# Linear attention and two dense stages on one core: queries of two halves through ScalarE and GpSimd, low part of y through TensorE in four halves

## The chip, the cores and the metric

The kernel runs on one core of a Trainium2 chip. The metric is the device time of one execution in microseconds (us). The kernel before took 769.47 us, the median of three runs (768.39, 769.47 and 771.44 us). A profiled execution of its own took 767.55 us.

## The reference

Three stages follow each other. The first is a gated linear attention, a recurrence over 768 steps for 4 batches and 8 heads of 48 dimensions:

```python
for t in range(S):
    state = alpha[:, :, t, :, None] * state + np.einsum('bhd,bhe->bhde', k[:, :, t], v[:, :, t])
    y[:, :, t] = np.einsum('bhd,bhde->bhe', q[:, :, t], state)
```

Its output, as 3072 tokens of 384 values, goes through a dense stage of 2048 hidden units with a rational function (`h = x @ w_in`, `g = P(h) / Q(h)`, `g @ w_out`), and then through one of 1024 hidden units with `h * softmax(h)`, a layer norm and `@ w_out`. Everything is float32.

## The kernel before, in words

**Numbers as two parts.** TensorE takes most operands as a pair: a rounded high part (`fp32r`) and the rest, the low part. A product of two such pairs takes three matmuls. So weights, activations and the attention's output y are all split: ScalarE copies the value to the high part, and another engine subtracts that from the value.

**The recurrence in chunks.** The 768 steps are cut into 6 chunks of 128. A *half* i is two of the four batches in one chunk, so there are 12 halves; chunk c has halves 2c and 2c+1. In a half, P is the running product of alpha from the chunk's start, and R is a scaled running product back from its end. The keys are multiplied by R and the queries by P. Then scores (line 421, tile `sc`), a causal mask (line 429 on GpSimd), and y as scores times v plus queries times the state (line 445, tile `y` in PSUM) follow, and last the state's update (tile `u`, line 486, and `Sbd`, lines 490 to 501).

**The first two halves** (`NPE = 2`) are prepared by `a_turn` (line 354): TensorE turns alpha, keys and queries by matmuls with the identity into PSUM (line 364). VectorE makes the scans for P (line 375) and R (line 379, with `zero` as its addend), and multiplies keys by R (line 383) and queries by P (line 384), each as one 128x512 instruction that reads PSUM. It does this for two groups p, so there are two of each per half. Later halves are prepared by `a_dve` (line 301), by VectorE's transposes (lines 291, 296), two scans (lines 309, 318) and products; there the queries are multiplied on GpSimd (line 336).

**y to the dense stage.** At the end of `a_pe` (lines 468 to 472) y lies in two PSUM tiles, of 512 and of 256 columns. For each, ScalarE copies the high part (line 471) and VectorE subtracts it from y, which gives the low part (line 472). All 12 halves do this, so there are 24 such subtractions. The PSUM tiles of the attention share two slots (tag `at`), and so the next tile that needs a slot waits until the last reader of an older one is done. Before halves 0 and 1 can update the state, `a_back` (line 393, tile `kp`) takes such a slot.

**The weights** of the first dense stage come in as pairs of 32-bit words (they are 64-bit in memory) and VectorE makes float32 of them in three instructions (lines 540, 543, 544), into a PSUM or SBUF buffer and then `ft`. ScalarE copies the high part (line 550) and GpSimd subtracts (line 551). This work, for four groups of hidden units, runs from the start of the kernel until about 139 us.

**The first dense stage** takes 16 units of hidden columns per chunk, 96 units in all. A unit u is `m_up` (9 matmuls, line 595; its function on ScalarE, VectorE and GpSimd, lines 600 to 629) and, four units later, `m_down` (9 matmuls, line 641). The PSUM tile `hp` of a unit has three slots. In the same loop, in pieces, run the halves from 2 on: the later halves are prepared and calculated while TensorE works on the units. The second dense stage (lines 709 to 799) comes behind this.

**What sets the order.** The program is written as one stream; a scheduler places it on the engines' queues by dependencies and a model of durations. Each engine then runs its queue strictly in order. `issue_after` adds, for instructions of the block on the same engine as the one named, an edge behind that one. At line 836 the preparation of half 2 is traced behind `marks[0, 1]`, which is the second subtraction of half 0 (line 472), a VectorE instruction:

```python
            with tc.issue_after(marks[0, 1].ins):
                _run(a_prep(2))
```

Other users of `issue_after` (lines 854 and 859 to 861) name instructions of the units. Before the loop the program is written in this order: loads of halves 0 and 1 with two pieces of the first weight group, `a_turn(0)`, `a_pe(0)`, `a_turn(1)`, `a_pe(1)`, the rest of that group, `clear()`, the second weight group, the preparation of half 2. All transfers are issued on SyncE's queue.

Of the kernel before, what the change touches and what calls it, by code (L numbers as in the profile page):

```python
# [7 lines left out]
F32 = mybir.dt.float32  # L8
F32R = mybir.dt.float32r
I32 = mybir.dt.int32  # L10
I64 = mybir.dt.int64
BF16 = mybir.dt.bfloat16
AF = mybir.ActivationFunctionType
ALU = mybir.AluOpType
# [5 lines left out]
def _view(ap, off, dims):  # L20
    return bass.AP(ap.tensor, ap.offset + off, [list(ap.ap[0])] + [list(d) for d in dims])
# [9 lines left out]
def kernel(  # L31
# [15 lines left out]
    nc = tc.nc  # L47
# [5 lines left out]
    CH = 128  # L53
# [9 lines left out]
    NPE = 2  # L63
# [90 lines left out]
    def network(fast):  # L154
# [7 lines left out]
        if fast:  # L162
            att = tc.tile_pool(name="att", bufs=1, side="right")
            ap_ = att.__enter__()
            ps_a = tc.tile_pool(name="ps_a", bufs=2, space=PSUM, side="right")
            ps_ap = ps_a.__enter__()
            ident = ap_.tile([128, 128], F32, name="ident")
            nc.gpsimd.memset(ident, 0.0)
            nc.gpsimd.affine_select(
                out=ident, in_=ident, pattern=[[-1, 128]], compare_op=ALU.not_equal, fill=1.0, base=0, channel_multiplier=1  # L170
            )
            zero = ap_.tile([128, CH], BF16, name="zero")
            nc.vector.memset(zero, 0.0)
            NB6 = 6
            PER = CH + 1
            QW = 4 * CH + 2
            d1 = ap_.tile([128, NB6 * PER + 1], BF16, name="d1")
            d2 = ap_.tile([128, NB6 * PER], F32, name="d2")
            alT = ap_.tile([128, NB6 * PER + 2], F32, name="alT")
            qks = ap_.tile([128, B, QW], F32, name="qks")  # L180
            kns = ap_.tile([128, B * 192 + 16], F32, name="kns")
            Sbd = ap_.tile([128, 2, B * 2, 2 * D], F32, name="Sbd")
            vns = ap_.tile([128, B * 256], F32, name="vns")

        def clear():
            nc.gpsimd.memset(d1, 0.0)
            nc.gpsimd.memset(_view(d1[:], 0, [[PER, NB6 + 1]]), 1.0)
            nc.gpsimd.memset(d2, 0.0)
            nc.vector.memset(alT[:, 0:1], 0.0)

# [35 lines left out]
        def half(i):  # L226
            if i not in halves:
                halves[i] = Half(i)
            return halves[i]

        marks = {}
# [3 lines left out]
        def watch(i, ra):  # L235
            jk = ap_.tile([128, 16 * D], BF16, name="jk", tag="qk")
            nc.scalar.activation(
                jk, ra[:, :16 * D], AF.Relu, bias=lim[:, 0:1], scale=-1.0, accum_out=bad[:, 2 * i:2 * i + 1]
            )

        def watch_end(i, end):
            jk = ap_.tile([128, 16], F32, name="jk2", tag="jk2")
            nc.scalar.activation(
                _view(jk[:], 0, [[end.shape[2], end.shape[1]], [1, end.shape[2]]]), end, AF.Relu, bias=lim[:, 1:2],
                accum_out=bad[:, 2 * i + 1:2 * i + 2],
            )
# [107 lines left out]
        def a_turn(i):  # L354
            hf = half(i)
            ra, rk, rq = raws.pop((i, "ra")), raws.pop((i, "rk")), raws.pop((i, "rq"))
            watch(i, ra)

            def turn(raw, p):
                t = (ps_hp if i < 2 else ps_ap).tile([128, B, CH], F32, name="tp", tag="h" if i < 2 else "at")  # L360
                for r in range(4):
                    for j in range(2):
                        o = (2 * p + j) * 192 + 48 * r
                        nc.tensor.matmul(
                            _view(t[64 * j:64 * j + 64], r, [[CH, B], [4, 32]]), lhsT=raw[:, o:o + 64], rhs=ident,
                            start=True, stop=True, skip_group_check=True,
                        )
                return t

            for p in range(2):  # L370
                al = turn(ra, p)
                P = ap_.tile([128, B, CH], F32, name="Pp", tag="P")
                R = ap_.tile([128, B, CH], F32, name="Rp", tag="qk")
                for b in range(B):
                    nc.vector.tensor_tensor_scan(P[:, b, :], al[:, b, :], zero, 1.0, ALU.mult, ALU.add)
                nc.vector.tensor_scalar(hf.end[p], P[:, :, CH - 1], P_MIN, None, ALU.max)
                nc.vector.reciprocal(R[:, :, CH - 1], hf.end[p])
                for b in range(B):
                    nc.vector.tensor_tensor_scan(
                        R[:, b, :CH - 1][:, ::-1], al[:, b, 1:][:, ::-1], zero[:, :CH - 1], R[:, b, CH - 1:],  # L380
                        ALU.mult, ALU.add,
                    )
                nc.vector.tensor_tensor(hf.k[p], turn(rk, p), R, ALU.mult)
                marks[i, p, 0] = nc.vector.tensor_tensor(hf.q[p], turn(rq, p), P, ALU.mult)
                yield
            watch_end(i, hf.ends[:, :, :, 0])

# [17 lines left out]
        def a_enter(i):  # L405
            if i < NPE:
                v_load(i)
                yield from a_turn(i)
            else:
                yield from a_move(i)  # L410

        def a_pe(i):
            c, bp = divmod(i, 2)
            vt = vts.pop(i)
            hf = half(i)
            A = {}
            for p in range(2):
                sc = [ps_ap.tile([128, B, CH], F32, name="sc", tag="at") for j in range(2)]
                for x in range(B):
                    for j in range(2):  # L420
                        nc.tensor.matmul(  # L421
                            sc[j][:, x, :],
                            lhsT=hf.k[p][64 * j:64 * j + D, x, :], rhs=hf.q[p][64 * j:64 * j + D, x, :],
                            start=True, stop=True,
# [13 lines left out]
            y2 = [ps_ap.tile([128, n, 2 * CH], F32, name="y", tag="at") for n in (2, 1)]  # L438
# [12 lines left out]
            for x in range(2):  # L451
                if c:
                    for hp in pairs:
                        g, p = divmod(hp, 2)
# [5 lines left out]
                for part in ((0, 1, 3), (2,)):  # L460
                    for hp in pairs:
                        g, p = divmod(hp, 2)
# [6 lines left out]
            for z, n in enumerate((2, 1)):  # L469
                hi, lo = (xt[:, 2 * z:2 * z + n, w, 256 * bp:256 * bp + 256] for w in range(2))  # L470
                nc.scalar.activation(hi, y2[z], AF.Copy)
                marks[i, z] = nc.vector.tensor_tensor(lo, y2[z], hi.bitcast(F32), ALU.subtract)
            yield
            if i >= NPE:
                yield
# [5 lines left out]
            for x in range(B):  # L481
                for p in range(2):
                    for j in range(2):
                        o = 192 * x + 96 * p + 48 * j
                        n = 256 * x + 128 * p + 64 * j
                        nc.tensor.matmul(
                            u[64 * j:64 * j + 64, 2 * x + p, :], lhsT=hf.kn[:, o:o + 64], rhs=vt[:, n:n + D],
                            start=True, stop=True, skip_group_check=True,
# [328 lines left out]
        if fast:  # L817
# [11 lines left out]
            take(pre, PRE[3])  # L829
            nc.gpsimd.memset(Sbd, 0.0)  # L830
            _run(a_turn(0), a_pe(0), a_turn(1), a_pe(1), pre)
            clear()
            pre = w1_group(1)
            take(pre, NA)
# [29 lines left out]
        def half_steps(i):  # L864
            gp = a_pe(i)
            gd = chain(a_prep(i + 1), a_move_qk(i + 1) if i + 1 >= NPE else iter(()), a_load(i + 2, ("ra", "rk")) if i + 2 < NH and i + 1 >= NPE else iter(())) if i + 1 < NH else iter(())
            while True:
                with pin(GP):
                    a = next(gp, "end")
                with pin(GS):  # L870
                    b = next(gd, "end")
                    if b != "end":
                        b = next(gd, "end")
                if a == "end" and b == "end":
                    if i + 1 < NH:
                        _run(a_enter(i + 1))
                        if i + 2 < NH and i + 1 < NPE:
                            _run(a_load(i + 2))
                    return
                yield  # L880
# [6 lines left out]
        for u in range(NU + LAG):  # L887
            c, f = divmod(u, NF1)
            now[0] = u
            if f % (NF1 // 2) == LATE and u < NU:  # L890
                _run(side)
                i = 2 * c + 2 + f // (NF1 // 2)
# [75 lines left out]
    def recurrence():  # L968
# [70 lines left out]
        sb.__exit__(None, None, None)  # L1039

    network(True)
    wide = nc.values_load(flag, min_val=0, max_val=1)
    with tc.If(wide > 0):
        recurrence()
        network(False)
# [30 lines left out]
```

## Time and profile before

| what | us |
|---|---|
| median of three runs | 769.47 |
| the profiled execution, its own time | 767.55 |
| its span, from the first to the last instruction | 765.8 |
| TensorE busy in the span | 726.4 |
| VectorE busy | 624.1 |
| ScalarE busy | 535.9 |
| GpSimd busy | 360.5 |

The profiled execution lies around its span by 1.75 us. In the rows, PE is TensorE's matmuls, PEld its loading of weights, DVE is VectorE, ACT is ScalarE, POOL is GpSimd, SP or SPq is SyncE's queue; L472 is line 472. A duration in the timeline runs until an instruction has fully ended, and the next one on the same engine may begin a little before that; so the step from one start to the next is the better price of an instruction in a queue that never waits.

### The profile page before, as it was taken

What the parts mean: (1) busy time and instruction counts of PE and PEld (TensorE: products, weight loads), DVE (VectorE), ACT (ScalarE), POOL (GpSimd) and SP (SyncE); (2) the same over time, 40 slices, a digit from 0 to 9 for tenths busy, and PEclk for the clock granted to TensorE, in tenths of its full rate; (3) what the DMA queues carried; (4) which work ended last, traced back from release to release, by engine and by line L of the source; (5) the groups of instructions that cost most, each with busy time, mean ns of one, the idle gap of its engine ahead of it and who ended that gap; (6) DMA issues with size and microseconds to landing.
All of it is one profiled execution on the core that took longest, in us unless ns stands there. A gap on an engine that the chain in (4) does not pass through costs nothing.

```text
span 765.8 us, 13905 instructions
## 1 busy us (share of the span) xinstructions
PE 726.4 (95%) x4976; PEld 606.0 (79%) x4976; DVE 624.1 (81%) x1111; ACT 535.9 (70%) x984; POOL 360.5 (47%) x306
## 2 busy tenths in 40 slices
PE   4775999999999999999999999999999999999996
PEld 4664777788888888877787878888888989988996
DVE  5999999879899999898989976568877787777730
ACT  2245877788888887897879798888875564645631
POOL 3256887766555455354444434422253334442422
PEclk9857899999999999999999999999999999999998
DMA  7995356357746584738462460910026264351552
GB/s 174 272 277 167 88 174 151 104 83 210 168 159 142 152 180 136 161 104 193 126 157 70 161 124 1 342 71 1 0 84 149 74 146 108 105 126 47 128 136 62
DMA packets 87278, 101.74 MB, mean 133 GB/s; under 512 B 34464, under 2 KB 63136, under 8 KB 87200
## 3 DMA queue, kind: packets, MB, share of 16 engines
q1 hardware_dynamic: 87008, 100.41, 49.9%
q8 instruction: 41, 0.67, 0.4%
q10 hardware_dynamic: 192, 0.36, 0.2%
q14 instruction: 37, 0.30, 0.1%
HBM read 60.59 MB, written 27.56 MB: 115 GB/s over the span
## 4 chain that ended last, share of the span: by engine, by line
PE 65%; DVE 20%; issue 5%; DMA 4%; ACT 3%; SPq 2%; POOL 0%; DVEq 0%; POOLq 0%; ACTq 0%
PE x2p L641 17%; PE hp L595 17%; PE op L787 13%; PE h L716 13%; PE y L445 2%; DMA lent<-in_moe_w_in_dram 2%; DVE w L624 2%; PE sc L421 2%; DVE hp L625 2%; SPq L267 2%; DVE p L626 1%; DVE ft L544 1%; DVE p L621 1%; DVE fp L543 1%; DVE qk L291 1%
## 5 line engine op out<-in xcount | busy, mean ns | idle before, releaser
L595 PE MATMUL hp<-xt,g 128*128 128x512 f32 x864 | 221.5, 399 | 14.8 <-DVE p L619 8.3
L629 POOL TENSOR_TENSOR gl<-p,gh 128x512 fp32r<-128x512 f32 x96 | 134.2, 1398 | 200.7 <-ACT gh L628 111.7
L595 PEld LDWEIGHTS hp<-xt,g 128*128 128x128 f32 x864 | 162.3, 191 | 55.5 <-DVE p L626 8.9
L641 PE MATMUL x2p<-gh,g 128*128 128x512 f32 x576 | 196.2, 396 | 0.4 <-ACT gh L628 0.4
L641 PEld LDWEIGHTS x2p<-gh,g 128*128 128x128 f32 x576 | 108.3, 189 | 26.1 <-ACT gh L628 1.2
L641 PE MATMUL x2p<-gl,g 128*128 128x512 f32 x288 | 113.2, 393 | 0.0
L779 POOL TENSOR_TENSOR room<-room,room 128x1024 fp32r<-128x1024 f32 x22 | 54.4, 2481 | 101.6 <-ACT room L778 84.1
L787 PE MATMUL op<-w2oh,room 128*128 128x384 f32 x384 | 101.5, 338 | 0.0
L624 DVE SCALAR_TENSOR_TENSOR w<-w,co,hp 128x512 f32<-128x512 f32 x84 | 61.7, 735 | 41.7 <-ACT hp L623 40.9
L716 PE MATMUL h<-w2ih,x 128*128 128x512 f32 x288 | 90.8, 394 | 0.0
L602 ACT ACTIVATE p<-hp,co 128x512 f32<-128x512 f32 x96 | 66.1, 689 | 12.6 <-POOL gl L629 11.8
L603 ACT ACTIVATE w<-ah,co 128x512 f32<-128x512 f32 x96 | 69.4, 724 | 6.1 <-DVE hp L625 5.8
L787 PEld LDWEIGHTS op<-w2oh,room 128*128 128x128 f32 x384 | 70.1, 188 | 0.9
L623 ACT ACTIVATE hp<-ah 128x512 f32<-128x512 f32 x84 | 50.2, 598 | 26.4 <-DVE p L621 25.5
L600 ACT ACTIVATE ah<-hp 128x512 f32<-128x512 f32 x96 | 57.0, 594 | 15.0 <-PE hp L595 14.6
L621 DVE SCALAR_TENSOR_TENSOR p<-p,co,hp 128x512 f32<-128x512 f32 x84 | 61.5, 732 | 5.6 <-ACT p L602 5.4
L787 PE MATMUL op<-w2ol,room 128*128 128x384 f32 x192 | 65.0, 339 | 0.0
L641 PEld LDWEIGHTS x2p<-gl,g 128*128 128x128 f32 x288 | 54.3, 188 | 11.9 <-issue 0.8
L628 ACT ACTIVATE gh<-p 128x512 fp32r<-128x512 f32 x96 | 59.9, 624 | 5.3 <-DVE p L626 2.5
L716 PEld LDWEIGHTS h<-w2ih,x 128*128 128x128 f32 x288 | 53.9, 188 | 11.8
L626 DVE SCALAR_TENSOR_TENSOR p<-p,co,hp 128x512 f32<-128x512 f32 x84 | 62.1, 740 | 1.0
L622 ACT ACTIVATE ah<-w,co 128x512 f32<-128x512 f32 x84 | 60.7, 723 | 1.0
(168 smaller groups left out, 1259.4 us busy)
## 6 DMA issues: line engine op xcount, KB each, us to landing
room<-room SPq DMA_DIRECT2D x94, 128.0 KB, 2.4
qk_d<-qk SPq DMA_DIRECT2D x10, 771.0 KB, 4.1
st<-in_moe_w_in_dram SPq DMA_DIRECT2D x13, 512.0 KB, 5.1
st<-in_moe_w_out_dram SPq DMA_DIRECT2D x16, 384.0 KB, 3.6
qks<-qk_d SPq DMA_DIRECT2D x20, 257.0 KB, 5.1
x<-x_d SPq DMA_DIRECT2D x18, 256.0 KB, 3.1
out_dram<-o SPq DMA_DIRECT2D x94, 48.0 KB, 1.6
ra<-in_alpha_dram SPq DMA_DIRECT2D x44, 96.0 KB, 2.8
```

What stands on the lines that cost most here:

```text
L595: last["PE", u] = nc.tensor.matmul(hp, lhsT=w[:, kt, 128 * o:128 * o + 128], rhs=xts[c][:, kt, xx, :], start=(kt == 0 and w is hi and xx = ...
L602: nc.scalar.activation(p, hp, AF.Square, bias=co[:, 7:8])
L603: nc.scalar.activation(w, ah, AF.Square, bias=co[:, 6:7])
L621: nc.vector.scalar_tensor_tensor(p, p, a1, hp, ALU.add, ALU.mult)
L622: nc.scalar.activation(ah, w, AF.Ln, bias=rest)
L624: nc.vector.scalar_tensor_tensor(w, w, rest, hp, ALU.add, ALU.mult)
L626: fin[u] = nc.vector.scalar_tensor_tensor(p, p, a0, hp, ALU.add, ALU.mult)
L628: last["ACT", u] = nc.scalar.activation(gh, p, AF.Copy)
L629: last["POOL", u] = nc.gpsimd.tensor_tensor(gl, p, gh[:].bitcast(F32), ALU.subtract)
L641: nc.tensor.matmul(x2ps[c][d], lhsT=w[:, o, 128 * d:128 * d + 128], rhs=gg, start=(f == 0 and w is hi and gg is gh), stop=(f == NF1 - 1 an ...
L716: nc.tensor.matmul(hp[:, 512 * n:512 * n + 512], lhsT=x2s[c][:, kt, x, CH * b:CH * b + CH], rhs=w2[w][:, kt, 512 * n:512 * n + 512], start ...
L787: nc.tensor.matmul(op, lhsT=x[:, 128 * f:128 * f + 128], rhs=w2[w][:, f, :], start=(f == 0 and x is hi and w == "oh"), stop=(f == NF2 - 1 ...
```

## The change

In halves 0 and 1 the turned queries are copied from PSUM by ScalarE into their SBUF place and multiplied there, in place, by P on GpSimd. In halves 0 to 3 (`i < NPE + 2`) the low part of y is made thus: TensorE multiplies the high part by minus the identity (tile `minus`, made once on ScalarE) and adds the product onto y in its PSUM tile, in one matmul of 256 columns for each of the three column groups; ScalarE then copies what is left. Halves 4 to 11 keep VectorE's subtraction. The tile `zero` becomes a part of `d1`, whose two fills on GpSimd are therefore written ahead of the first halves and not in `clear()`.

```diff
-            zero = ap_.tile([128, CH], BF16, name="zero")
-            nc.vector.memset(zero, 0.0)
+            minus = ap_.tile([128, 128], F32R, name="minus")
+            nc.scalar.activation(minus, ident, AF.Copy, scale=-1.0)
...
+            nc.gpsimd.memset(d1, 0.0)
+            nc.gpsimd.memset(_view(d1[:], 0, [[PER, NB6 + 1]]), 1.0)
+            zero = d1[:, 1:1 + CH]
...
         def clear():
-            nc.gpsimd.memset(d1, 0.0)
-            nc.gpsimd.memset(_view(d1[:], 0, [[PER, NB6 + 1]]), 1.0)
...
-                marks[i, p, 0] = nc.vector.tensor_tensor(hf.q[p], turn(rq, p), P, ALU.mult)
+                nc.scalar.activation(hf.q[p], turn(rq, p), AF.Copy)
+                marks[i, p, 0] = nc.gpsimd.tensor_tensor(hf.q[p], hf.q[p], P, ALU.mult)
...
                 nc.scalar.activation(hi, y2[z], AF.Copy)
-                marks[i, z] = nc.vector.tensor_tensor(lo, y2[z], hi.bitcast(F32), ALU.subtract)
+                if i < NPE + 2:
+                    for a in range(n):
+                        nc.tensor.matmul(
+                            y2[z][:, a, :], lhsT=minus, rhs=hi[:, a, :], start=False, stop=True, skip_group_check=True
+                        )
+                    marks[i, z] = nc.scalar.activation(lo, y2[z], AF.Copy)
+                else:
+                    marks[i, z] = nc.vector.tensor_tensor(lo, y2[z], hi.bitcast(F32), ALU.subtract)
```

## Rows read from the trace of the kernel before

**Rows 1.** The page: TensorE and VectorE in 40 equal slices, busy tenths.
```profile
PE   4775999999999999999999999999999999999996
...
DVE  5999999879899999898989976568877787777730
```

**Rows 2.** Waits of TensorE, 0 to 80, 80 to 150, 150 to 766 us: total, times, longest.
```profile
PE hp L595 <- DVE p L619: 8.3, 1, 8.3
PE kp L393 <- DVE xt L472: 4.1, 2, 3.2
PE hp L595 <- ACT xt L471: 2.5, 1, 2.5
...
PE hp L595 <- DVE p L626: 2.5, 2, 1.3
...
PE hp L595 <- DVE p L626: 1.3, 4, 0.4
```

**Rows 3.** Windows: busy us of PE, PEld, DVE, ACT, POOL, then clock, DMA share, GB/s.
```profile
20.00:30.00 10.00, 8.36 (x117) 6.77 (x116) 9.94 (x32) 2.52 (x5) 2.46 (x3) 0.82 1.12 298
30.00:40.00 10.00, 6.61 (x100) 5.81 (x92) 10.00 (x24) 3.70 (x9) 2.85 (x4) 0.86 1.03 250
...
80.00:90.00 10.00, 10.00 (x45) 7.93 (x44) 10.00 (x19) 8.60 (x16) 7.07 (x8) 0.92 0.45 132
```

**Rows 4.** Timeline of VectorE (start us, us), 15 to 18 us, with the idle time before.
```profile
15.63 0.17 DVE L127 TENSOR_SCALAR bad<-co 128x2 f32<-128x2 f32 x1 [1.37 <-ACT co L118]
...
16.50 0.68 DVE L384 TENSOR_TENSOR qks<-tp,Pp 128x512 f32<-128x512 f32 x1
17.55 0.69 DVE L540 TENSOR_SCALAR fp<-lent 128x512 int32<-128x512 int32 x1 [0.36 <-DMA lent<-in_moe_w_in_dram]
```

**Rows 5.** Groups of VectorE's instructions by line, 0 to 76.7 us: busy us, mean ns.
```profile
L472 DVE TENSOR_TENSOR xt<-y,xt 128x512 fp32r<-128x512 f32 (+1 forms) x4 | 2.1, 533 | 0.0
...
L384 DVE TENSOR_TENSOR lent<-tp,Pp 128x512 f32<-128x512 f32 x2 | 1.3, 674 | 0.0
...
L291 DVE STREAM_TRANSPOSE alT<-ra 128x256 f32<-128x256 f32 x2 | 1.3, 651 | 0.0
```

**Rows 6.** Timeline of VectorE (start us, us): steps of lines 384 and 472.
```profile
35.17 0.65 DVE L472 TENSOR_TENSOR xt<-y,xt 128x512 fp32r<-128x512 f32 x1
35.75 0.67 DVE L384 TENSOR_TENSOR lent<-tp,Pp 128x512 f32<-128x512 f32 x1
36.35 0.41 DVE L472 TENSOR_TENSOR xt<-y,xt 128x256 fp32r<-128x256 f32 x1
...
117.10 1.01 DVE L472 TENSOR_TENSOR xt<-y,xt 128x512 fp32r<-128x512 f32 x2
118.03 1.60 DVE L543 SCALAR_TENSOR_TENSOR ft<-st,ft 128x384 int32<-128x384 int32 x1
```

**Rows 7.** Timelines of VectorE and GpSimd: three small instructions, what GpSimd ran then.
```profile
23.96 0.16 DVE L376 TENSOR_SCALAR end<-Pp 128x4 f32<-128x4 f32 x1
...
25.43 0.88 DVE L137 TENSOR_TENSOR co<-co 128x2 f32<-128x2 f32 x1
...
33.07 1.18 DVE L376 TENSOR_SCALAR end<-Pp 128x4 f32<-128x4 f32 x1
...
25.02 1.28 POOL L551 TENSOR_TENSOR g<-ft,g 128x512 fp32r<-128x512 f32 x1 [5.42 <-ACT g L550]
...
32.96 1.26 POOL L551 TENSOR_TENSOR g<-ft,g 128x512 fp32r<-128x512 f32 x1 [5.49 <-ACT g L550]
```

**Rows 8.** Timeline of TensorE at units 3 and 4, with the idle time before.
```profile
76.70 4.21 PE L595 MATMUL hp<-xt,g 128*128 128x512 f32 x9 [8.28 <-DVE p L619]
...
83.20 2.21 PE L595 MATMUL hp<-xt,g 128*128 128x512 f32 x9
```

**Rows 9.** Timeline of ScalarE: a copy out of a unit's tile, both copies of y.
```profile
110.08 0.68 ACT L602 ACTIVATE p<-hp,co 128x512 f32<-128x512 f32 x1
...
113.26 0.86 ACT L471 ACTIVATE xt<-y 128x512 fp32r<-128x512 f32 x2
```

## The prediction, made before the changed kernel was run

> **What bounds the kernel now.** I read the slices of the page first [rows 1]. VectorE is full from slice 2 on, that is from 19 us, while TensorE is full only from slice 5 on, near 77 us (a slice is 19.1 us). So there is an opening of some 77 us in which VectorE has hardly a pause and TensorE is fed by it, and a long rest in which TensorE has no pause. The waits of TensorE say the same [rows 2]: its longest, 8.3 us, is in the opening, for a VectorE instruction of the first unit (line 619), and it ends at 76.70 us [rows 8]. From 80 to 150 us TensorE waits 2.5 us for line 626, again on VectorE; from 150 us to the end, 1.3 us in all. What the opening saves is therefore kept to the end, since nothing behind it has room to eat it up, and what is added to TensorE behind 77 us is paid in full.
>
> Once its work has begun, VectorE waits for others mostly at its start: 1.37 us for a ScalarE instruction and 0.36 us for weights, both before 18 us [rows 4], and next to nothing from there to 80 us. The windows from 20 to 40 us show VectorE at 9.94 and 10.00 of 10, ScalarE and GpSimd at a quarter to a third, and the transfers full at 1.12 and 1.03 [rows 3]. The change takes work from VectorE where it is scarce and gives it to engines that have time there; what has to be priced is how much of VectorE's time is really on the path.
>
> **The change part by part.** A VectorE instruction in a queue without pauses costs the step to the next start: from 35.17 to 35.75 is 0.58 us for an instruction of 0.65, and from 35.75 to 36.35 is 0.60 for one of 0.67 [rows 6]. So a step is about 0.07 us less than the duration.
>
> *Queries of half 1.* Two multiplications of 0.674 us [rows 5] leave VectorE: 2 x 0.60 = 1.2 us saved.
>
> *Queries of half 0.* Two more of 0.68 us, the later at 16.50 us, in a stretch in which VectorE waits 1.7 us anyway [rows 4]. If the waits are fixed by transfers, removal only lengthens them: 0. If other ready work moves into the hole, 1.2. I take the middle, 0.6.
>
> *Low part of y, halves 0 and 1.* Four subtractions of 0.533 us on average [rows 5], at a step of 0.46 each: 1.8 saved.
>
> *Low part, halves 2 and 3.* Half 2's pair at 117.10 us takes a step of 0.93 us [rows 6], between units that share VectorE with weight work. TensorE is the bound there, but its waits for line 626 (2.5 us in all, the longest 1.3) are VectorE's lateness, so this can be had where a wait follows. I credit one pair, 0.9; the ends are 0 and both pairs, 1.85.
>
> *Multiplications on GpSimd.* Four are added, each like a 128x512 subtraction on GpSimd, 1.28 us [rows 7]. GpSimd is busy 2.5 to 2.9 us of 10 there, and the scores that need the queries stand far behind them, so by itself this is hidden. But it costs VectorE something: a VectorE instruction on 4 numbers, 0.16 us at 23.96 us, takes 1.18 at 33.07, just while GpSimd runs its subtraction from 32.96 on, and another small one takes 0.88 at 25.43, until GpSimd's of 25.02 ends [rows 7]. So small VectorE instructions are held until the GpSimd one is through. Two such cases, 1.02 + 0.72 = 1.74 us, stand in 20 us in which GpSimd was busy 2.46 + 2.85 = 5.31 us [rows 3]: a third of GpSimd's time is lost on VectorE. Half 1's two multiplications are 2.56 us, which makes 0.8 us; half 0's fall where VectorE waits, so 0. The ends are 0 and, if each of the four holds up VectorE for its whole length, 5.1. The Trainium skill says of this (SBUF — State Buffer, Who interferes with whom) that GpSimd and VectorE's second port share one lock, held for a whole instruction, and that a VectorE instruction with two SBUF inputs, or in a two-port mode, fully blocks against a GpSimd one that reads SBUF. The trace agrees, with 1.18 us in place of 0.16; the rule speaks against the multiplication on GpSimd, whose two inputs are both in SBUF, and for the removed one, which had one of them in PSUM.
>
> *The matmuls by minus the identity.* Three of 256 columns per half, 12 in all. Nine of 512 columns take 2.21 us at the full clock [rows 8], so one of 256 about 0.12. The six of halves 0 and 1 lie in TensorE's idle time, such as the 8.3 us; should that cover go, they are 0.7. The six of halves 2 and 3 are on the path: 0.7 us paid.
>
> *Waits that these add.* The matmul needs ScalarE's high copy, and it stands in TensorE's queue, with units' matmuls behind it. Half 1's first unit shows such a wait now, 2.5 us for line 471 [rows 2], where there was nothing else to run. From 80 to 150 us TensorE shows no wait for ScalarE, though each unit's `m_down` depends on it: the queue has other matmuls to put between. I take 0; the end above is rival 2.
>
> *ScalarE's work.* It gets four query copies and eight low copies; a pair like that is 0.86 us [rows 9], so 4 x 0.86 plus 4 x 0.6, some 6 us. It is idle by three quarters from 20 to 30 us, and at 8.60 of 10 from 80 to 90 us [rows 3]. In the opening I cost that at 0; in the loop it is under rival 2.
>
> *Slots.* TensorE waits 4.1 us in the opening until line 472 frees a slot for `kp` [rows 2]. A low part that doesn't stand in VectorE's queue frees it sooner. VectorE sets the pace behind that wait, so I credit 0.
>
> *Order.* The named instruction at line 836 becomes a ScalarE one, so VectorE's preparation of half 2 loses its edge, and its transposes (two large ones, 1.3 us [rows 5], and two smaller) may come before half 1's scans. VectorE's sum up to 76.7 us stays, so 0; at worst half 1 comes 2.6 us later. ScalarE's two checks of half 2 get the edge; nothing of a unit stands behind them that early. The fills of `d1` come forward on GpSimd; VectorE's first scan still waits for TensorE's turned alpha. No transfer is added or moved; those that wait for VectorE go a little sooner.
>
> *The sum:* -1.2 - 0.6 - 1.8 - 0.9 + 0.8 + 0.7 = -3.0 us. The profiled execution took 767.55 us (a span of 765.8 and 1.75 around it), so the same execution would be 764.5. The median of the runs, 769.47, stands 1.9 above it, and the forecast on that scale is 766.5 us.
>
> **The rivals.** (1) *VectorE's whole sum counts.* All four multiplications (2.4) and four pairs (3.7) are on the path, nothing is held up, and only TensorE's 0.7 is paid: -5.4, 764.1 us. For it: VectorE has hardly a pause from 20 to 80 us. Against it: TensorE alone is the bound in most of the stretch of halves 2 and 3. If in addition the first units start sooner since y's low part is ready sooner, the 2.5 us wait goes too: 761.6.
>
> (2) *TensorE waits on ScalarE in the loop; slower.* At four places (halves 2 and 3, two tiles each) TensorE stands until ScalarE's high copy is through, which stands behind one unit's first three instructions, at 0.68 us each [rows 9]: 2.0 us a place, 8.2 in all, which with the -3.0 makes +5.2, 774.7 us. It decides from 0.75 us a place on. For it: ScalarE is at 8.60 of 10. Against it: no such wait in the rows now, and other matmuls are there to be put between.
>
> (3) *The freed time is not on the path.* The transfers are full from 20 to 40 us [rows 3], and VectorE runs into its weights: what is saved before about 38 us is waited away. Only half 1's subtractions (0.9) and half 2's (0.9) count, less 0.7: 768.4. Against it: VectorE's last wait for weights lies before 18 us.
>
> (4) *GpSimd holds up VectorE in full.* With 5.1 us in place of 0.8 the sum is +1.3, 770.8 us. This is what the lock of the page named above would make if each multiplication met a VectorE instruction of the kind that it blocks. Against it: most VectorE instructions there read one operand from PSUM or write to it, and those run at their usual length.
>
> **How the numbers follow.** A measurement of this kernel can tell about 0.5% (3.85 us) from no change. The forecast gets 0.32, rival 1 0.30, rival 2 0.12, rival 3 0.18, rival 4 0.08. Faster by more than 3.85 us (below 765.6): 0.28 of rival 1 and 0.13 of the forecast, whose credit for halves 0, 2 and 3 has open ends, makes 0.41. Slower by more (above 773.3): 0.11 of rival 2 and 0.02 of rivals 3 and 4, 0.13. Within: 0.46. The range goes from 761.5, rival 1 with its further gain, to 771.5, just beyond rival 4; rival 2 is left out.
>
> **What would show it.** VectorE's list up to the loop has no line 384 and no subtraction before chunk 2; the 8.3 us wait ends at 73 to 74 us where it now ends at 76.7. TensorE's waits from 80 to 150 us name VectorE for under 2.5 us. Rival 1 shows a start before 72 us; rival 2 shows waits of the new matmuls for line 471's copy, of 0.75 us or more each; rival 3 shows VectorE pausing for weights between 18 and 40 us; rival 4 shows small VectorE instructions of over 1 us beside the new multiplications. I am wrong if the loop starts as forecast and the end doesn't follow, for then the rest of the kernel has room that the waits don't show.

## The result, and the profile after

The changed kernel takes **774.99 us** (median of seven runs, 772.69 to 775.66); the kernel before took 769.37 beside it (seven runs). The ratio is 1.0066, with a 95% interval of 1.0048 to 1.0084: slower, where 766.5 was forecast. The profiled execution after took 774.51 us with a span of 772.8, and before 767.55 with 765.8, so the two profiles are 7.0 us apart.

I followed the same instructions through both traces. The changed kernel is ahead at the loop's start, behind by 165 us, and its VectorE is behind by more at 634 us. (The *loop* is the stretch from about 80 to 165 us in which units and halves run side by side.) The opening first: the page's slices after (those of rows 1), and the timeline of TensorE after (that of rows 8).

```profile
PE   5866997999999999999999999999999999999986
...
DVE  5998999969999999898989976667878797877730
```

```profile
74.36 4.21 PE L604 MATMUL hp<-xt,g 128*128 128x512 f32 x9 [6.81 <-DVE p L628]
...
110.98 0.52 PE L476 MATMUL y<-xt,minus 128*128 128x256 f32 x3
...
126.34 3.92 PE L604 MATMUL hp<-xt,g 128*128 128x512 f32 x9 [5.16 <-DVE alT L304]
```

The wait before the fourth unit ends at 74.36 us, 2.3 us sooner than at 76.70 [rows 8]. The same unit matmuls are 2.3 us ahead at 80 us and 1.8 us behind at 165 us: **the first loss, 4.1 us, lies in the loop.** The last row has a new wait of 5.16 us, and the nine matmuls behind it take 3.92 us where nine take 2.21 at the full clock [rows 8]. Here are TensorE's waits after, from 0 to 80 us and from 80 to 168 us (total, times, longest), as in rows 2.

```profile
PE hp L604 <- DVE p L628: 6.8, 1, 6.8
...
PE kp L395 <- ACT xt L479: 2.0, 2, 1.4
PE y L476 <- ACT xt L473: 1.4, 1, 1.4
...
PE hp L604 <- DVE alT L304: 5.2, 1, 5.2
PE hp L604 <- DVE p L635: 1.0, 3, 0.4
```

From 80 to 168 us that is 6.2 us of waits. Before it was 3.1: the 2.5 of rows 2, and this one, for the state's update:

```profile
PE sc L421 <- DVE Sbd L496: 0.6, 1, 0.6
```

Line 304, which the 5.2 us wait names, is a memset of 0.07 us that ended at the same moment as what TensorE needed: VectorE's last instruction of unit 8 (line 628, 619 before). Two timelines of VectorE lead up to it, first of the kernel after:

```profile
114.25 0.74 DVE L622 SCALAR_TENSOR_TENSOR hp<-p,co,hp 128x512 f32<-128x512 f32 x1
114.91 1.01 DVE L549 TENSOR_SCALAR ft<-st 128x384 int32<-128x384 int32 x1
115.96 1.54 DVE L552 SCALAR_TENSOR_TENSOR ft<-st,ft 128x384 int32<-128x384 int32 x1
117.53 0.93 DVE L553 SCALAR_TENSOR_TENSOR ft<-st,ft 128x384 int32<-128x384 int32 x1
120.03 0.36 DVE L549 TENSOR_SCALAR ft<-st 128x384 int32<-128x384 int32 x1 [1.57 <-DMA st<-in_moe_w_out_dram]
...
121.98 1.50 DVE L553 SCALAR_TENSOR_TENSOR ft<-st,ft 128x384 int32<-128x384 int32 x1
...
124.45 1.23 DVE L552 SCALAR_TENSOR_TENSOR ft<-st,ft 128x384 int32<-128x384 int32 x1
125.61 0.68 DVE L628 SCALAR_TENSOR_TENSOR p<-w,hp 128x512 f32<-128x512 f32 x1
```

And of the kernel before:

```profile
119.55 0.68 DVE L619 SCALAR_TENSOR_TENSOR p<-w,hp 128x512 f32<-128x512 f32 x1
...
120.82 0.55 DVE L544 SCALAR_TENSOR_TENSOR ft<-st,ft 128x384 int32<-128x384 int32 x1
...
122.75 0.68 DVE L543 SCALAR_TENSOR_TENSOR ft<-st,ft 128x384 int32<-128x384 int32 x1
```

Unit 8's last instruction starts at 125.61 us in place of 119.55. The scheduler has put the last weight pieces earlier in VectorE's queue. Before, pieces 26 and 27 of the 28 (three instructions each) stood behind unit 8's last instruction; now they stand ahead of it, all but the last instruction of 27, and so do the first two of piece 28 ahead of unit 9's. One of them waits 1.57 us for its transfer, and VectorE's instructions with two SBUF inputs (`ft<-st,ft`) last long: 0.54 us at best, 1.54, 1.50 and 1.23 here. The groups of VectorE from 94 to 146 us (busy us, mean ns) show it, of before and then of after:

```profile
L543 DVE SCALAR_TENSOR_TENSOR ft<-st,ft 128x384 int32<-128x384 int32 (+1 forms) x7 | 6.7, 952 | 0.1
L540 DVE TENSOR_SCALAR ft<-st 128x384 int32<-128x384 int32 (+1 forms) x7 | 5.4, 765 | 0.0
L544 DVE SCALAR_TENSOR_TENSOR ft<-st,ft 128x384 int32<-128x384 int32 (+1 forms) x7 | 5.1, 723 | 0.0
```

```profile
L552 DVE SCALAR_TENSOR_TENSOR ft<-st,ft 128x384 int32<-128x384 int32 (+1 forms) x7 | 9.1, 1294 | 0.1
L553 DVE SCALAR_TENSOR_TENSOR ft<-st,ft 128x384 int32<-128x384 int32 (+1 forms) x7 | 6.8, 971 | 0.1
L549 DVE TENSOR_SCALAR ft<-st 128x384 int32<-128x384 int32 (+1 forms) x7 | 5.1, 725 | 1.6 <-DMA st<-in_moe_w_out_dram 1.6
```

Twenty-one of these instructions take 21.0 us after and 17.2 before. Below I call VectorE's *excess* what its instructions in a stretch take beyond the shortest of the same line and shape in that trace. From 105 to 135 us it is 5.1 us before and 9.5 after. Over the whole loop, from 80 to 168 us, it is 10.7 and 15.0.

**The second loss lies in VectorE's queue at 621 to 634 us**, in the second dense stage. VectorE is 2.8 us behind the kernel before ahead of it and 7.7 behind after it, 4.9 us more; 0.5 of that is a longer wait for a transfer at 625 us. The timelines of VectorE and GpSimd, of after and then of before:

```profile
627.40 2.35 DVE L762 SCALAR_TENSOR_TENSOR sm<-sm 128x1 f32<-128x1 f32 x1
629.79 3.02 DVE L763 TENSOR_SCALAR room<-room,sm 128x1024 f32<-128x1024 f32 x1
...
627.33 4.92 POOL L788 TENSOR_TENSOR room<-room,room 128x1024 fp32r<-128x1024 f32 x2 [0.18 <-ACT room L787]
```

```profile
624.12 0.16 DVE L753 SCALAR_TENSOR_TENSOR sm<-sm 128x1 f32<-128x1 f32 x1
624.32 0.81 DVE L754 TENSOR_SCALAR room<-room,sm 128x1024 f32<-128x1024 f32 x1
...
624.84 2.56 POOL L779 TENSOR_TENSOR room<-room,room 128x1024 fp32r<-128x1024 f32 x1 [0.96 <-ACT room L778]
```

Before, GpSimd paused 0.96 us between two subtractions, and VectorE's two instructions slipped through in 0.16 and 0.81 us. After, it goes on within 0.18 us, and the same two take 2.35 and 3.02. ScalarE's copies ahead of the two subtractions, which wait for transfers, began 3.36 us apart before (620.34 and 623.70 us) and 2.59 apart after (623.61 and 626.20).

TensorE feels this only at the end. It stays 2.8 us behind until 747 us, and then comes the one wait that it has behind 600 us (before it has none):

```profile
747.10 0.44 PE L796 MATMUL op<-w2oh,room 128*128 128x384 f32 x1 [2.41 <-ACT room L787]
```

Behind it the granted clock falls (0.83 on average from 745 to 755 us, 1.00 in the ten us on either side), which is another 1.7 us. So about 4.1 us of the 7.0 at the end come from here, and 2.8 from the loop and what follows it.

### The profile page after: what moved, and what is told of

It reads as the page before. It is cut to its first block, busy times and chain, and to the rows that moved or that the text cites. A ratio compares the mean times of both kernels' runs of the same rounds, so it can differ in the third digit from the quotient of the medians.

```text
span 772.8 us, 13924 instructions
## 1 busy us (share of the span) xinstructions
PE 729.8 (94%) x4988; PEld 607.2 (79%) x4988; DVE 627.7 (81%) x1098; ACT 540.1 (70%) x997; POOL 363.9 (47%) x310
## 4 chain that ended last, share of the span: by engine, by line
PE 38%; DVE 29%; DMA 9%; ACT 9%; issue 7%; SPq 5%; POOL 2%; ACTq 0%; DVEq 0%; POOLq 0%
PE hp L604 15%; PE x2p L650 15%; DVE room L765 3%; SPq L777 3%; PE op L796 2%; ACT jk L750 2%; DVE room L748 2%; DMA room<-room 2%; DVE room L763 2%; DVE sm L744 2%; DVE w L633 2%; PE sc L423 2%; DVE hp L634 2%; PE h L725 2%; PE y L447 2%
## 5 line engine op out<-in xcount | busy, mean ns | idle before, releaser
L788 POOL TENSOR_TENSOR room<-room,room 128x1024 fp32r<-128x1024 f32 x22 | 54.1, 2466 | 100.0 <-ACT room L787 83.4
L611 ACT ACTIVATE p<-hp,co 128x512 f32<-128x512 f32 x96 | 66.0, 687 | 12.4 <-POOL gl L638 11.7
L725 PEld LDWEIGHTS h<-w2ih,x 128*128 128x128 f32 x288 | 53.9, 188 | 11.7
```

The costliest lines, as they stand in the source:

```text
L611: nc.scalar.activation(p, hp, AF.Square, bias=co[:, 7:8])
L725: nc.tensor.matmul(hp[:, 512 * n:512 * n + 512], lhsT=x2s[c][:, kt, x, CH * b:CH * b + CH], rhs=w2[w][:, kt, 512 * n:512 * n + 512], start ...
```

## The experiments

The main theory at first: VectorE is the bound in the loop too, and what it was spared in the opening is lost there to weight pieces queued sooner, GpSimd's hold and late transfers; the second loss is GpSimd's hold again. The rival: TensorE's own new work in the loop, or its waits for ScalarE, cost it. Where the fourth unit's wait ends is called *start* (76.70 us before, 74.36 after). The loop's length is the time from matmul 36 to matmul 288 of the units, those of `m_up` and `m_down` counted together from 0 (84.0 us before, 88.1 after).

**How far one profile can be trusted.** Each kernel has one profile, but some kernels have queues that are the same, instruction for instruction, up to 620 us, since they differ only in the second dense stage. Their loops measure 84.0 and 85.4 us (before), 88.1 and 89.3 (after), 87.1 and 85.5 (after, with the order mended, below) and 83.1 and 83.4 (the quickest kernel, below). I call such kernels twins. A difference under some 1.6 us between two loops shows nothing by itself. VectorE's excess from 105 to 135 us differs by up to 1.8 us in such pairs (5.1 and 6.9 before), and from 80 to 168 us by 0.3 at most.

**Each part alone.** In this order: the queries only, the low part only (queries again on VectorE), and the change with the low part in halves 0 and 1 only.

```diff
-                if i < NPE + 2:
+                if i < 0:
```

```diff
-                nc.scalar.activation(hf.q[p], turn(rq, p), AF.Copy)
-                marks[i, p, 0] = nc.gpsimd.tensor_tensor(hf.q[p], hf.q[p], P, ALU.mult)
+                marks[i, p, 0] = nc.vector.tensor_tensor(hf.q[p], turn(rq, p), P, ALU.mult)
```

```diff
-                if i < NPE + 2:
+                if i < NPE:
```

> Only the queries of halves 0 and 1 go through ScalarE and GpSimd; every low part of y is VectorE's subtraction again. The changed kernel's trace stands 2.3 us ahead at the loop's start, 2.8 us behind from unit 30 on, and 6.8 us behind from the second stage's 12th tile on. Theory A, that the weights of the last group are now queued where GpSimd holds VectorE up (VectorE's excess over its shortest durations from 105 to 135 us rose from 5.1 to 9.5 us): without the low part's edits the queue of the loop falls back towards the one of before, unit 30 is within 1 us of before or ahead, and the end is 0 to 2 us faster than before unless the second stage loses its 4 us again. Theory B, that TensorE's new matmuls and ScalarE's second copies in halves 2 and 3 cost the loop its 5 us: the same here, since they are gone. Theory C, that any shift of the opening loses as much: unit 30 is 2 to 3 us behind as in the changed kernel.

> Only the low part of y in halves 0 to 3 goes through TensorE and ScalarE; the queries of halves 0 and 1 are multiplied on VectorE again. Theory A: the loss follows the queue, so if the last weight group is again pulled ahead, unit 30 is 2 to 4 us behind, with VectorE's excess from 105 to 135 us near 9 us; if not, it is level. Theory B: unit 30 is 3 to 4 us behind, whatever the queue, and VectorE's excess stays near 5 us. Theory C: 2 to 3 us behind with no pattern in the excess.

> The whole change, but the low part goes through TensorE in halves 0 and 1 only; halves 2 and 3, which run inside the loop, keep VectorE's subtraction. Theory B: the gain of 2.3 us at the loop's start is kept, unit 30 is about 2 us ahead of before, the end 2 us faster or, with the second stage's loss, 2 us slower. Theory A: the loss depends on where the last weight group stands; if it stands as in the changed kernel, unit 30 is 2 to 3 us behind though the matmuls in the loop are gone.

Queries only: 778.0 us, ratio 1.0106 [1.0073, 1.0138], start 80.37. Low part only: 772.76, 1.0046 [1.0028, 1.0064], start 78.06. So neither part alone makes the start sooner (profiles with the opening of before start at 76.70 to 78.01), and together they do: the parts don't add. With the queries alone, TensorE's waits and VectorE's, from 0 to 80 us and a little beyond, are:

```profile
PE kp L395 <- DVE xt L481: 5.8, 2, 3.2
...
DVE fp L549 <- ACT lent L399: 4.7, 1, 4.7
DVE fp L549 <- DMA lent<-in_moe_w_in_dram: 2.1, 1, 2.1
```

What VectorE was spared it waited away, for the PSUM slots (tag `at`) that weight pieces share with `kp`: ScalarE's copy of `kp` (line 399) frees one, and `kp` itself waits for its own until VectorE's late subtraction (line 481) is through. Low part in halves 0 and 1 only: 773.99, 1.0049 [1.0029, 1.007]; the loop is 88.0 us long with none of TensorE's new work in it. So that work isn't needed for the loss. Nor is it needed that pieces 26 and 27 stand ahead of unit 8's last instruction: here it starts at 124.5 us, and piece 26's last two instructions at 125.1 and 126.7. The loss comes as waits, most of them for VectorE (from 80 to 168 us, with the other three 8.8 us):

```profile
PE hp L604 <- DVE p L635: 2.9, 4, 1.4
PE hp L604 <- DVE p L628: 2.9, 1, 2.9
PE sc L423 <- issue: 1.9, 1, 1.9
```

**The second loss.** Piece 5 of the second stage is subtracted on VectorE, so GpSimd has a pause there.

```diff
-    FASTS = (0, 20)
+    FASTS = (0, 5, 20)
```

> The whole change, and in the second dense stage one more of the 24 tiles (number 5) has its low part made by VectorE, not GpSimd. In the changed kernel that tile's two neighbours run back to back on GpSimd for 4.92 us from 627.33 us and two VectorE instructions take 2.35 and 3.02 us instead of 0.16 and 0.81. Theory: the second loss, 4.0 us from the second stage's 12th tile on, is GpSimd holding VectorE. Then it goes here: the offset stays at +2.8 us (a new VectorE instruction of about 1.3 us may cost a part), and the time is 3 to 4 us under the changed kernel's. Rival, that the loss comes from transfers or from TensorE: it stays at 6.8 us.

771.62 us, 1.0018 [1.0, 1.0037], 3.4 us under the changed kernel. From 511 to 634 us it loses nothing (4.6 us behind at either end), and TensorE's wait at 747 us is gone: the second loss is this hold. The same edit in the kernel before, which has no such loss:

> The kernel before, with tile 5's low part in the second stage on VectorE. If the second loss of 3 to 4 us is a matter of when transfers land, which the kernel before escapes in its profile, then its own trace has nothing to gain there: the time stays within 1 us of before, and its spread over runs may shrink. If instead the kernel before also loses it in many timed runs: 1 to 3 us faster in the median.

769.63, 0.9983 [0.9963, 1.0003]: no difference that can be told.

**Order and holds.** Weight pieces stay behind the units (one a unit after the fourth, and the last behind the last VectorE instruction of units 8 to 10):

```diff
-                    if f % 4 == 0:
+                    if f % 4 == 0 and f != 8:
                         _run(prep)
...
-                    with later(G1):
-                        take(prep, 1)
+                    with later(G1):
+                        take(prep, 1 if u < 4 else 0)
                 m_up(u)
                 if fast and u < NF1:
-                    with later(G1):
+                    with tc.issue_after(fin[u].ins) if u >= 8 else later(G1):
                         take(prep, 1)
```

> The whole change, with VectorE's queue put back in one place: the last weight group's pieces are traced one per unit, and the last three come behind the last VectorE instruction of units 8, 9 and 10, so that unit 8 stands ahead of two pieces and unit 9 ahead of one, as in the kernel before. Theory A1 (queue order: pieces ahead of units 8 and 9 make TensorE wait 5.2 us for a slot near 121 us, and that is never made good): that wait shrinks under 2 us, unit 30 and the first tile of the second stage are 1 to 3 us ahead of before, and the end, with the second stage's loss of 4 us, 1 to 3 us slower than before. Theory A2 (GpSimd holds up VectorE whatever the order): VectorE's excess from 105 to 135 us stays at 8 to 9 us and the first tile of the second stage 2 to 3 us behind.

772.77, 1.0036 [1.0012, 1.006]. The 5.2 us wait is gone (the longest is 2.2). The loop is 87.1 us, and 85.5 in its twin, against 88.1 and 89.3: some 2.4 of the 4.0 us are back on average. In the other direction, the kernel before with edges that put pieces ahead of the last instruction of units 8 and 9 (`wl[x]` counts from 0 and is the instruction of line 544 of a piece, so `wl[26]` is piece 27's; the same with `wl[27]` for unit 9):

```diff
-                fin[u] = nc.vector.scalar_tensor_tensor(p, w, 2.0, hp, ALU.subtract, ALU.mult, reverse0=True)
+                with tc.issue_after(wl[26].ins) if u == 8 else ExitStack():
+                    fin[u] = nc.vector.scalar_tensor_tensor(p, w, 2.0, hp, ALU.subtract, ALU.mult, reverse0=True)
```

> The kernel before with nothing of the change, but with two edges that keep the last VectorE instruction of units 8 and 9 behind pieces 27 and 28 of the weights, which brings the pieces ahead of these units as in the changed kernel. Theory A1: TensorE waits 4 to 7 us near 120 us, the first tile of the second stage is 3 to 6 us behind, the end 3 to 6 us slower (more if the second stage loses its tile too). Theory A2: under 2 us lost by unit 30, unless VectorE's excess from 105 to 135 us rises over its 5.1 us.

772.52, 1.0039 [1.0014, 1.0065], VectorE's excess from 105 to 135 us up from 5.1 to 8.9. Its opening came out 2.5 us later too (its queue differs from 16 us on), which is most of its loss. The loop is 85.2 us, no longer than the 84.0 and 85.4 of the kernel before, and TensorE's longest wait in it is 1.9. So theory A1 fails here: putting the pieces ahead raises the holds, but is not shown to make the loop longer by itself.

Now GpSimd's reads are taken away in units 5 to 9 (low parts filled with zeros by a memset, which reads nothing), in the changed kernel, with the pieces behind the units as well, and in the kernel before.

```diff
-            last["POOL", u] = nc.gpsimd.tensor_tensor(gl, p, gh[:].bitcast(F32), ALU.subtract)
+            if fast and 4 < u < 10:
+                last["POOL", u] = nc.gpsimd.memset(gl[:].bitcast(F32), 0.0)
+            else:
+                last["POOL", u] = nc.gpsimd.tensor_tensor(gl, p, gh[:].bitcast(F32), ALU.subtract)
```

> The whole change, with the low part of the units' activations left out in units 5 to 9: GpSimd fills it with zeros in place of its subtraction, so five GpSimd instructions that read SBUF are gone from 105 to 135 us, while pieces 26 and 27 still stand ahead of unit 8 in VectorE's queue. Theory A2: VectorE's excess from 105 to 135 us falls from 9.5 to about 5 us and the loop's loss of 5 us to 1 or 2. Theory A1: the excess may fall, but the loss of 3 us or more from the loop's start to the first tile of the second stage stays.

> Both earlier edits together: units 8 to 10 ahead of the last three weight pieces, and zeros in place of the low part of the units' activations in units 5 to 9 (that part is left out). From the loop's start to the first tile of the second stage the changed kernel lost 5.1 us, the units-first order alone 4.1, the zeros alone 4.6; with the zeros VectorE's excess fell to 3.8 us but it then waited 5.3 us for weights. Theory D (VectorE is the bound until 150 us, and what is freed goes to the next of three: GpSimd's holds, weights not yet there, pieces ahead of units): with holds and order both mended the loss falls to 1 us or less, the first tile is 1 to 2 us ahead of before. Rival E (the loss is TensorE's own: new matmuls, lower clock after a wait): 3 us or more stay lost.

> The kernel before with only the zeros in units 5 to 9 (the low part of those activations is left out). Theory D: VectorE is the bound here too, so its excess of 5.1 us from 105 to 135 us falls to 1 to 3 us and the first tile of the second stage comes 1 to 3 us sooner than before, or, if weights are then missing, VectorE shows a new wait for them. Rival E: no change of the loop, within 0.5 us.

The first took 772.73 us, 1.004 [1.0019, 1.0061]: excess down from 9.5 to 3.8, loop 86.9. So most of the excess is GpSimd's reads; but VectorE, with pieces still ahead of unit 8, now waited for its transfers, 5.3 us in place of 1.6:

```profile
L552 DVE SCALAR_TENSOR_TENSOR ft<-st,ft 128x384 int32<-128x384 int32 (+1 forms) x7 | 6.1, 878 | 0.1
...
L549 DVE TENSOR_SCALAR ft<-st 128x384 int32<-128x384 int32 (+1 forms) x7 | 3.3, 478 | 5.3 <-DMA st<-in_moe_w_out_dram 5.3
```

With the order mended too: 769.6, 0.9981 [0.9959, 1.0002], loop 83.8, no longer than that of the kernel before (it still lost 3 us between 165 and 511 us, whose cause I didn't find, and 3.1 at 626). The kernel before without the reads: 766.69, 0.997 [0.9928, 1.0012], no difference that can be told in the time, loop 81.8. So GpSimd's holds cost both kernels, and with them away from both the changed kernel's loop is still 5.1 us longer (86.9 and 81.8). The holds alone are therefore not the difference. With the order mended as well it is 2.0 longer, near what twins differ by. How the order of VectorE's queue, its transfers and the holds share the first loss is not shown beyond this.

**Together.** The changed kernel with the mended order and piece 5, then the same with the low part in halves 2 and 3 back on VectorE:

> As the run before it, and tile 5's low part in the second stage on VectorE too, which took away the second loss in an earlier run. Theory A1: both losses gone, the opening's gain is left: 1 to 3 us faster than before, near 767 us. Theory A2: as the run with that tile alone, 771 to 772 us.

> Queries of halves 0 and 1 on GpSimd, low part by TensorE in halves 0 and 1 only, units 8 to 10 ahead of the last pieces, tile 5 on VectorE. Against the run with the same order and tile but four halves (768.9 us): 0.7 us of TensorE's matmuls less, one VectorE pair more ahead of TensorE's waits. Theory D: about the same, 768 to 770 us. Rival E: 1 us or more faster, under 768.

768.89 us, 0.9984 [0.9963, 1.0005], loop 85.5; and **765.06 us, 0.9927 [0.9897, 0.9956]**, loop 83.1, quicker than both kernels. Both wait 4.0 us in all from 80 to 168 us (their twins 4.7 each). The waits that I compare, of the first and then of the second:

```profile
PE hp L604 <- DVE p L635: 1.4, 4, 0.4
PE y L447 <- POOL A L431: 1.0, 1, 1.0
PE hp L604 <- DVE p L628: 1.0, 1, 1.0
PE x2p L650 <- POOL gl L638: 0.6, 1, 0.6
```

```profile
PE hp L604 <- DVE p L635: 2.4, 4, 1.4
PE hp L604 <- DVE p L628: 0.7, 1, 0.7
PE y L447 <- POOL A L431: 0.6, 1, 0.6
PE y L447 <- ACT A L430: 0.3, 1, 0.3
```

So moving halves 2 and 3 shortened no wait. It added six matmuls, and with them the granted clock fell once, at 131 us (nine matmuls in 3.81 us). Without them the clock stayed full. The twins agree, with a fall at 145 us and with none; but the kernel without GpSimd's reads and with the order mended has the six matmuls and no fall, so they are not shown to cause it. Windows from 84 to 164 us, the clock third from the end, of the first and of the second:

```profile
84.00:164.00 80.00, 76.07 (x588) 59.56 (x587) 73.66 (x111) 59.11 (x111) 60.31 (x52) 0.98 0.50 129
```

```profile
84.00:164.00 80.00, 75.80 (x593) 58.55 (x594) 74.22 (x118) 61.22 (x113) 62.30 (x54) 1.00 0.53 134
```

Last, whether the change has a gain of its own in this: the kernel before with the same two edits and nothing of the change, beside the quickest again.

> The kernel before, with the two edits of the quickest kernel that are no part of the change (weight pieces behind units 8 to 10, GpSimd's first turn in the second stage at piece 5). Theory: up to the loop VectorE is the bound and the change's first two halves take 2 to 3 us off it, so this kernel without them stays within 1.5 us of before (768 to 770 us, ratio 0.998 to 1.001) with a fourth unit's wait that ends at 75.5 to 77.5 us. Rival: the gain of the quickest kernel is the two edits' own, and this one reaches 765 to 766 us too.

> The quickest kernel again, beside the one before it, on the same chip. Theory: ratio 0.990 to 0.996, the fourth unit's wait ends at 73.5 to 75.5 us, no fall of the granted clock from 84 to 164 us, and TensorE's waits there come to about 4 us. Rival: the first result was a lucky arrival of transfers; then the ratio is 0.997 or more and either the clock falls once in the loop or the waits are over 6 us.

The kernel before with the edits took 772.6 us, 1.003 [1.0011, 1.005]; the quickest 765.23, 0.9936 [0.9914, 0.9958], on the same chip. The gain isn't the edits'. TensorE's timelines at the fourth unit, without the change and with it:

```profile
77.53 4.21 PE L595 MATMUL hp<-xt,g 128*128 128x512 f32 x9 [8.48 <-DVE p L619]
```

```profile
74.44 3.90 PE L604 MATMUL hp<-xt,g 128*128 128x512 f32 x9 [6.86 <-DVE p L628]
```

3.1 us sooner (2.9 in the first run of the quickest, 74.62). The rest of the 7 us is the loop again, 88.2 against 83.4 us. So the edits that shorten the changed kernel's loop make that of the kernel before longer (84.0 and 85.4 without them), though pieces 26 to 28 stand behind units 8 and 9 in both. They suit one kernel's queue and not the other's; why isn't shown.

**What makes the loop's length.** I added TensorE's waits from 80 to 168 us, what the clock's falls cost (from 84 to 164 us in slices of 8, each slice times one less the granted clock) and the new matmuls, at a step of 0.12 us each (three take from 110.98 to 111.34 us):

| kernel | loop | waits | clock | matmuls | rest |
|---|---|---|---|---|---|
| before | 84.0 | 3.1 | 1.7 | 0 | 79.2 |
| before, piece 5 (twin) | 85.4 | 3.3 | 3.4 | 0 | 78.7 |
| after | 88.1 | 6.2 | 1.7 | 0.7 | 79.5 |
| after, piece 5 (twin) | 89.3 | 6.8 | 3.4 | 0.7 | 78.4 |
| low part in halves 0, 1 | 88.0 | 8.8 | 0 | 0 | 79.2 |
| after, order and piece 5 | 85.5 | 4.0 | 1.8 | 0.7 | 79.0 |
| the quickest | 83.1 | 4.0 | 0 | 0 | 79.1 |
| the quickest again (twin) | 83.4 | 4.7 | 0 | 0 | 78.7 |
| before, order and piece 5 | 88.2 | 6.0 | 3.4 | 0 | 78.8 |

The rest is the same within 1.1 us here; in the other kernels it is 78.3 to 79.9, and 77.0 to 77.5 in three, in part since idle time at a low clock is counted twice. So the 4.1 us between before and after are 3.1 of waits, nearly all for VectorE, 0.7 of new matmuls and 0.3 of rest. Their twins say the same: 3.9 us, of which 3.5 are waits.

## Why the prediction was wrong

**The failed step** is in the first part: "What the opening saves is therefore kept to the end, since nothing behind it has room to eat it up". It took TensorE for the only bound from 77 us on, since it waited 2.5 us for VectorE from 80 to 150 us [rows 2]. But VectorE was at 10.00 of 10 from 80 to 90 us [rows 3]: the two were nearly level, and a loss of VectorE's became a wait of TensorE's. The runs showed the opposite of what the step says: 2.3 us ahead at the loop's start became 1.8 behind at its end, with TensorE's waits up from 3.1 to 6.2 us, and the second loss put a wait of 2.4 us and a fall of the clock near the end, where the trace before had no wait at all. The prediction itself had named the sign, a loop that starts as forecast and an end that doesn't follow. It weighed the order of VectorE's queue for the opening only, at 0; the order in the loop, which the scheduler makes anew, was no term of the sum.

**Opening.** Forecast -1.2, -0.6, -1.8 and +0.8, that is -2.8; measured -2.3, and -2.9 and -3.1 against the kernel before with the same two edits. Profiles with one and the same opening differ by up to 1.6 us here, but they don't overlap: the four with the opening of before start at 76.70 to 78.01 us, the nine with the change's at 74.36 to 75.92, on average 2.5 sooner. The size was right, though the single terms aren't shown by it: neither part alone made the start sooner. The credit of 0.6 for half 0 has no row of its own. The wait of `kp` fell from 4.1 us [rows 2] to 2.0.

**Low part in halves 2 and 3.** Forecast -0.9 for VectorE and +0.7 for six matmuls. The price of the matmuls was right, a step of 0.12 us each. The credit was not: TensorE waits as long with them as without (4.0 us, and 4.7 in the twins).

**GpSimd's hold.** It was costed at 0.8 us, beside the new multiplications only. In the opening VectorE's excess hardly rose (8.0 us before and 8.2 after, from 0 to 76 us); in the loop it rose by 4.3 us (80 to 168 us), and at 627 us the hold cost VectorE 4.4 more. The mechanism was right, its places were not.

The Trainium skill has a rule for the two-input instructions at these places (SBUF — State Buffer, Who interferes with whom): a VectorE instruction with two SBUF inputs contends with a GpSimd one that reads SBUF, not with one that only writes it, and the one that issues first holds the ports for its whole length. The runs agree: an excess of 9.5 us from 105 to 135 us with the subtractions (8.7 in the twin) and of 3.8 with a memset in their place.

**The rivals.** Rival 1 (a start before 72 us): no, 74.36. Rival 2 (TensorE waits on ScalarE in the loop) had the right size, 774.7, and the wrong cause: the new matmuls wait 1.4 us in all, before 80 us. Rival 3 (weights): in part; VectorE waits 0.91 us at 11.7 and 0.94 at 17.4 us for weights, where it was 0.36 [rows 4] at the second, but not between 18 and 40 us. Rival 4 (GpSimd holds VectorE in full beside its multiplications): no, the excess in the opening rose by 0.2 us, and the small instruction that took 1.18 us [rows 7] takes 0.78.

**Open.** Why VectorE comes late in the loop, beyond the one wait of 5.2 us that the trace ties to the weight pieces ahead of unit 8; why the same edits of the order help the changed kernel and hurt the kernel before; why the changed kernel falls 1.1 us further behind between 309 and 365 us; and why VectorE in all seven kernels with the change, or a part of it, and without the edit of piece 5 lost 2.8 to 5.0 us between 511 and 634 us, and in none of the three of the kernel before without it.

## What to carry to other kernels

Where two engines are both full, a short list of waits on one doesn't make it the only bound: a few us more in the other's queue, or a new order in it, can show up as waits. Work taken off an engine under a scheduler changes the order of all that stands behind it, so compare the queues of both kernels before believing a sum of durations. And with GpSimd beside VectorE, price every VectorE instruction with two SBUF inputs along the way, not only those next to the new work. With its low part in halves 0 and 1 only and two more edits, this change came out 0.6 to 0.7% quicker than the kernel before; neither the change nor the two edits alone did. And measure the spread between profiles of the same queue before reading a difference of a microsecond or two in one of them.

## What the runs showed of the hardware

Back-to-back GpSimd subtractions let VectorE through only between them: an instruction on 128x1 took 2.35 us in place of 0.16, and the one of 128x1024 behind it 3.02 in place of 0.81, while GpSimd's two ran on in 4.92. And the granted clock fell to the lower of its two levels in the loop behind a wait of 5.16 us (nine matmuls in 3.92 us at 126.34), but also behind one of 0.38 us (3.81 us at 131.16 in the kernel with order and piece 5 mended), and not in the loop of the kernel with the low part in halves 0 and 1 only, which has 8.8 us of waits in all, the longest 2.90.
